# Three buffers for the second layer's operand sums and for raw weights, and six sums and two folds held to their written place on VectorE

## The chip, the cores and the metric

The kernel runs on one core of one Trainium2 chip. The metric is the device time of one execution in microseconds, as the median of several runs. Engines are called by the profile's names: PE (TensorE), DVE (VectorE), ACT (ScalarE), POOL (GpSimd) and SP (SyncE, which here only issues transfers).

## The reference, cut to what matters

Four batches, eight heads, 576 tokens, head size 64. An attention onto 32 packed tokens and back gives x (2304 x 512). Two feed-forward layers follow:

```python
def _moe_ref(x, w_in, w_out):              # 512 -> 2048 -> 512
    h = x @ w_in
    g = np.maximum(h, 0.0) + np.log1p(np.exp(-np.abs(h)))
    return (g @ w_out).astype(np.float32)

def _moe2_ref(x, w_gate, w_val, w_out):    # 512 -> 1536 -> 512
    gate = 1.0 / (1.0 + np.exp(-(x @ w_gate)))
    val = x @ w_val
    return (gate * val @ w_out).astype(np.float32)
```

The activations are float32. The five weight matrices arrive as 64-bit floats, 8 bytes an element.

## The kernel before, in words

**Stages.** Attention units (batch, group of four heads) run at the head of the program, mixed with the first chunks of layer 1. Layer 1 goes over entries (batch, chunk of 256 hidden columns): `emit_h` computes a chunk of h, `emit_out1` multiplies it with w_out, and DVE adds the product into `xa`, the resident activation (line 682). The last chunks are done for batches 0 and 1 first, then for 2 and 3. Layer 2 goes over two passes of two batches each (`ps` 0 and 1) and, in each, over 12 steps `f` of 128 hidden columns: `emit_gv` computes gate and value, `emit_out2` multiplies them with the output weights for two steps together and DVE adds the product into `xa` (line 1030).

**Products.** Every float32 operand is cut into a high part (rounded by ACT or POOL, `hi_of` and `split`) and a low part (x minus the high part, `split_lo`, line 101, on DVE or POOL), and a product is three matmuls (`mm3`, lines 113 to 115). In layer 2 a 2 x 2 block scheme with seven products is used: on the activation's side the seven operands are A11, A12, A22 (quarters of x) and S1 to S4 (sums of quarters). `prep_A(b)` makes them for batch b: a sum on DVE (`sum_` and `tt`, line 711), its high part on ACT (line 737), its low part on DVE or POOL (`ALO`), and so on. For batches 0 and 1 the chain is S1 = x21 + x22, S2 = S1 - x11, S4 = x12 - S2, S3 = x11 - x21. For batches 2 and 3 `fold_A` first writes two of the sums into `xa` in place (two instructions a batch), and `prep_A` then makes three more (S3, S1, S4). `prep_A(0)` and `prep_A(1)` are written into the end of layer 1, `fold_A(2)` and `fold_A(3)` into steps f = 3 and f = 5 of pass 0 or just behind them, `prep_A(2)` and `prep_A(3)` into the end of pass 0.

**The buffer of the sums.** A sum goes into a tile with the tag "sum" of the pool `w2[0]`, which has one buffer for it. S2 and S4 of batches 0 and 1 are written in place into the tile that holds S1.

**Raw weights.** A block of weights (512 KB) is loaded by SP into a tile of the pool `raw`, which has `NRAW` = 2 buffers (`load_next`), and DVE turns it into float32 by three integer instructions (`convert`, lines 180, 185, 189). Each conversion writes the next load into the program behind it; four loads are written at the start. `prep_B` prepares the weights of one step of layer 2: three conversions, four block sums on POOL (lines 800 to 803), splits, and four or five transfers that keep the blocks for pass 1 (line 816). Pass 1 reads them back (line 835).

**Order.** Background work (`jobs`) is written in small steps between the matmul groups by `tick`. The order on each engine and on SP isn't the written one, though: the framework plans it before the run from its own estimate of durations, and an instruction whose operands and buffer are free may be placed ahead of work written before it. `keep_in_program_order` ties an instruction behind the one written just before it on its engine, and makes it wait for nothing else. At run time each engine executes its list strictly in order.

Of the kernel before, what the change touches and what calls it, by code (L numbers as in the profile page):

```python
# [9 lines left out]
F32 = mybir.dt.float32  # L10
# [4 lines left out]
ALU = mybir.AluOpType  # L15
# [6 lines left out]
def attn_moe_moe_kernel(  # L22
# [21 lines left out]
    nc = tc.nc  # L44
# [5 lines left out]
    P = 128  # L50
    NC = 6
    CT = S // NC
    HS = S // 2
# [1 line left out]
    NCH1 = F1 // CF  # L55
    NCH2 = F2 // CF
    KD = DM // P
    NRAW = 2
    CPS = 1
    CPC = (1, 2)  # L60
    TP = 1
# [18 lines left out]
    big = ctx.enter_context(tc.tile_pool(name="big", bufs=11))  # L80
    raw = ctx.enter_context(tc.tile_pool(name="raw", bufs=NRAW))
    cv = ctx.enter_context(tc.tile_pool(name="cv", bufs=NCV))
# [17 lines left out]
    def split_lo(eng, lo, x, hi):  # L100
        eng.tensor_tensor(lo, x, hi.bitcast(F32), op=ALU.subtract)  # L101
# [599 lines left out]
    w2 = []  # L701
    NF = NCH2 * 2
    HB = B // 2
    Aop, Bop, scratch, gv = {}, {}, {}, {}

    def quarters(b):
        x1, x2_ = x2(b, 0), x2(b, 1)
        return x1[:, :2], x1[:, 2:], x2_[:, :2], x2_[:, 2:]

    def tt(to, x, y, op):  # L710
        nc.vector.tensor_tensor(to, x, y, op=op)

    def fold_A(b):

        x11, x12, x21, x22 = quarters(b)
        tt(x21, x21, x22, ALU.add)
        yield
        tt(x21, x21, x11, ALU.subtract)
        yield

    def prep_A(b):

        pool = w2[0] if b % 2 == 0 else big
        n = 11 if pool is big else 7
        Aop[b] = {}
        for nms in (("A11", "S2"), ("S3", "S1"), ("A12", "A22"), ("S4",)):
            tiles = [
                pool.tile([P, 2, 2, HS], F32R, tag="big", bufs=n, name="aop")
                for _ in range(len(nms))
            ]  # L730
            for e, nm in enumerate(nms):
                Aop[b][nm] = [tiles[0][:, e], tiles[-1][:, 1 if len(nms) == 1 else e]]
        x11, x12, x21, x22 = quarters(b)

        def split(nm, x):
            hi, lo = Aop[b][nm]
            nc.scalar.activation(hi, x, AF.Copy)  # L737
            split_lo(nc.gpsimd if nm in ALO[b] else nc.vector, lo, x, hi)

        def sum_(x, y, op, to=None):  # L740
            if to is None:
                to = w2[0].tile([P, 2, HS], F32, tag="sum", name="sum")
            tt(to, x, y, op)
            return to

        if b >= HB:

            steps = [
                ("A11", x11), ("S2", x21), ("S3", x22, x21, ALU.subtract),
                ("S1", x21, x11, ALU.add), ("A12", x12), ("A22", x22),  # L750
                ("S4", x12, x21, ALU.subtract),
            ]
            for nm, *x in steps:
                if len(x) > 1:
                    x = [sum_(*x)]
                    yield
                split(nm, x[0])
                yield
            return
        for nm, x in (("A11", x11), ("A12", x12), ("A22", x22)):  # L760
            split(nm, x)
            yield
        t = sum_(x21, x22, ALU.add)
        yield
        split("S1", t)
        yield
        sum_(t, x11, ALU.subtract, t)
        yield
        split("S2", t)
        yield  # L770
        sum_(x12, t, ALU.subtract, t)
        yield
        split("S4", t)
        yield
        t = sum_(x11, x21, ALU.subtract)
        yield
        split("S3", t)
        yield
# [101 lines left out]
    for i, (b, c) in enumerate(entries):  # L880
# [10 lines left out]
        if c >= 2 and b % 2 == 0:  # L891
# [3 lines left out]
            if k + 1 < len(groups):  # L895
                x, cc = groups[k + 1]
# [12 lines left out]
        for x in range(2):  # L909
            if (b, c) == (x + 2, NCH1 - 2):  # L910
                jobs.append((f"A{x}", prep_A(x)))
# [139 lines left out]
    for i, (ps, f) in enumerate(steps):  # L1051
        finish(f"B{ps}{f}")
        if i + 1 < len(steps):
            n_ps, n_f = steps[i + 1]
            jobs.append((f"B{n_ps}{n_f}", prep_B(n_ps, n_f)))
        if ps == 0 and f in FOLD:
            jobs.append((f"F{FOLD[f]}", fold_A(FOLD[f])))
        whole = list(range(HB))
        first_last = f in (SPL if ps else (SP0 + [NF - 1]))
        for n, group in enumerate([[p] for p in whole] if first_last else [whole]):  # L1060
            for p in group:
                finish(f"A{HB * ps + p}")
            emit_gv(ps, f, group)
            if ps == 0 and f == NF - 1:
                jobs.appendleft((f"A{HB + n}", prep_A(HB + n)))
            some_out2(LEFT if n or not first_last else LEFT0)
        if f % 2:
            todo.extend((ps, f // 2, t) for t in range(NTT))
            spread[0] = -DEL
# [37 lines left out]
```

## Time and profile before

| | |
|---|---|
| median of 3 runs | 865.22 us (864.93 to 866.91) |
| profiled execution, its own time | 869.49 us |
| its span, first to last instruction | 867.7 us |
| PE busy | 846.9 us, 98% |
| DVE busy | 587.9 us, 68% |
| POOL busy | 475.8 us, 55% |
| ACT busy | 339.8 us, 39% |
| mean granted clock of TensorE | 0.993 |

PE is busy nearly all the time, so what counts is where it stands still or is clocked lower, and which engine it waits for there. Layer 1 ends at about 439 us, pass 0 of layer 2 at about 642 us. Matmul ends are modelled by the profiler.

### The profile page before, as it was taken

What the parts mean: (1) busy time and instruction counts of PE and PEld (TensorE: products, weight loads), DVE (VectorE), ACT (ScalarE), POOL (GpSimd) and SP (SyncE); (2) the same over time, 40 slices, a digit from 0 to 9 for tenths busy, and PEclk for the clock granted to TensorE, in tenths of its full rate; (3) what the DMA queues carried; (4) which work ended last, traced back from release to release, by engine and by line L of the source; (5) the groups of instructions that cost most, each with busy time, mean ns of one, the idle gap of its engine ahead of it and who ended that gap; (6) DMA issues with size and microseconds to landing.
All of it is one profiled execution on the core that took longest, in us unless ns stands there. A gap on an engine that the chain in (4) does not pass through costs nothing.

```text
span 867.7 us, 15523 instructions
## 1 busy us (share of the span) xinstructions
PE 846.9 (98%) x6112; PEld 794.4 (92%) x6112; DVE 587.9 (68%) x1004; ACT 339.8 (39%) x626; POOL 475.8 (55%) x453
## 2 busy tenths in 40 slices
PE   7899999999999999999899999999999999999997
PEld 5789989999999999999889999999988999999996
DVE  1785566956365646646788687887897746667665
ACT  4367665554433434444433332222352432322210
POOL 4364333245655545575669786876984634436400
PEclk9899999999999999999999999999999999999999
DMA  9974321203033402400054655744515413213003
GB/s 227 209 207 117 83 56 29 74 25 99 1 98 92 135 12 87 127 26 1 1 177 146 188 152 149 207 132 128 163 51 151 115 47 90 67 43 110 13 1 109
DMA packets 58023, 85.53 MB, mean 99 GB/s; under 512 B 6368, under 2 KB 39264, under 8 KB 57952
## 3 DMA queue, kind: packets, MB, share of 16 engines
q1 hardware_dynamic: 56944, 83.31, 34.3%
q10 hardware_dynamic: 1008, 1.25, 0.4%
q8 instruction: 48, 0.79, 0.4%
q14 instruction: 23, 0.19, 0.1%
HBM read 65.67 MB, written 18.87 MB: 97 GB/s over the span
## 4 chain that ended last, share of the span: by engine, by line
PE 83%; DVE 8%; DMA 3%; ACT 2%; POOL 2%; issue 2%; SPq 0%; POOLq 0%; ACTq 0%; DVEq 0%
PE bank L115 8%; PE bank L113 8%; PE bank L114 8%; PE ps L674 7%; PE ps L675 7%; PE ps L677 7%; PE ps L1022 5%; PE ps L1023 5%; PE ps L1024 5%; PE ps L113 4%; PE ps L115 4%; PE ps L114 4%; PE ps L603 2%; PE ps L478 2%; PE ps L362 1%
## 5 line engine op out<-in xcount | busy, mean ns | idle before, releaser
L113 PE MATMUL bank<-aop,BH 128*128 128x288 f32 x672 | 199.2, 296 | 3.0 <-DVE work L987 1.1
L115 PE MATMUL bank<-aop,BL 128*128 128x288 f32 x672 | 198.9, 296 | 0.0
L114 PE MATMUL bank<-aop,BH 128*128 128x288 f32 x672 | 198.0, 295 | 0.2 <-DVE aop L101 0.2
L682 DVE TENSOR_TENSOR xa<-xa,ps 128x288 f32<-128x288 f32 x224 | 100.3, 451 | 105.8 <-PE ps L677 105.4
L101 POOL TENSOR_TENSOR ghl<-g,ghl 128x576 fp32r<-128x576 f32 x64 | 93.3, 1458 | 134.7 <-ACT ghl L108 125.2
L674 PE MATMUL ps<-ghl,woh 128*128 128x288 f32 x512 | 149.6, 307 | 2.6 <-DVE xa L682 2.4
L675 PE MATMUL ps<-ghl,wol 128*128 128x288 f32 x512 | 144.4, 297 | 0.0
L113 PEld LDWEIGHTS bank<-aop,BH 128*128 128x128 f32 x672 | 126.3, 188 | 8.7 <-issue 2.1
L114 PEld LDWEIGHTS bank<-aop,BH 128*128 128x128 f32 x672 | 126.6, 188 | 4.1 <-DVE aop L101 0.4
L115 PEld LDWEIGHTS bank<-aop,BL 128*128 128x128 f32 x672 | 126.6, 188 | 0.2 <-POOL BL L101 0.2
L101 POOL TENSOR_TENSOR BL<-cv,BH 128x512 fp32r<-128x512 f32 (+1 forms) x96 | 118.2, 1246 | 3.6 <-ACT BH L108 2.4
L677 PE MATMUL ps<-ghl,woh 128*128 128x288 f32 x512 | 109.5, 295 | 0.0
L674 PEld LDWEIGHTS ps<-ghl,woh 128*128 128x128 f32 x512 | 97.0, 189 | 5.1 <-ACT aop L737 2.1
L675 PEld LDWEIGHTS ps<-ghl,wol 128*128 128x128 f32 x512 | 97.2, 190 | 0.6
L975 DVE TENSOR_TENSOR work<-work,bank 128x576 f32<-128x576 f32 (+1 forms) x100 | 70.8, 724 | 30.7 <-PE bank L115 29.8
L1022 PE MATMUL ps<-oh,gv 128*128 128x512 f32 x216 | 84.5, 391 | 1.0 <-DVE xa L1030 0.5
L1023 PE MATMUL ps<-ol,gv 128*128 128x512 f32 x216 | 85.0, 393 | 0.0
L1024 PE MATMUL ps<-oh,gv 128*128 128x512 f32 x216 | 84.9, 394 | 0.0
L677 PEld LDWEIGHTS ps<-ghl,woh 128*128 128x128 f32 x512 | 82.7, 189 | 0.0
L1030 DVE TENSOR_TENSOR xa<-xa,ps 128x512 f32<-128x512 f32 x90 | 61.5, 684 | 28.8 <-PE ps L1024 28.4
L113 PE MATMUL ps<-A2h,wph 128*128 128x288 f32 x256 | 77.6, 303 | 0.3 <-ACT wph L587 0.3
L115 PE MATMUL ps<-A2h,wpl 128*128 128x288 f32 x256 | 76.3, 298 | 0.4 <-DVE wpl L101 0.4
(131 smaller groups left out, 1594.5 us busy)
## 6 DMA issues: line engine op xcount, KB each, us to landing
cv<-B SPq DMA_DIRECT2D x52, 256.0 KB, 2.7
B<-cv SPq DMA_DIRECT2D x48, 256.0 KB, 4.0
raw_in<-in_moe_w_in_dram SPq DMA_DIRECT2D x16, 512.0 KB, 3.9
raw_out<-in_moe_w_out_dram SPq DMA_DIRECT2D x16, 512.0 KB, 3.6
raw_g<-in_moe_w_gate_dram SPq DMA_DIRECT2D x12, 512.0 KB, 4.1
raw_v<-in_moe_w_val_dram SPq DMA_DIRECT2D x12, 512.0 KB, 4.5
raw_o<-in_moe_w_out_dram SPq DMA_DIRECT2D x12, 512.0 KB, 4.1
xa<-in_q_dram SPq DMA_DIRECT2D x6, 576.0 KB, 6.9
```

The source lines that it names most:

```text
L101: eng.tensor_tensor(lo, x, hi.bitcast(F32), op=ALU.subtract)
L113: nc.tensor.matmul(ps, wh, xh, start=first, stop=False)
L114: nc.tensor.matmul(ps, wh, xl, start=False, stop=False)
L115: nc.tensor.matmul(ps, wl, xh, start=False, stop=last)
L674: nc.tensor.matmul(out_, wh[:, ms], gh[:, f], start=f == 0, stop=False)
L675: nc.tensor.matmul(out_, wl[:, ms], gh[:, f], start=False, stop=False)
L677: nc.tensor.matmul(out_, wo_hl[c, f][0][:, ms], gl[:, f], start=False, stop=f == 1)
L682: nc.vector.tensor_tensor(dst, dst, out_, op=ALU.add)
L975: nc.vector.tensor_tensor(to, x, y, op=ALU.add)
L1022: nc.tensor.matmul(bank, gh[:, ts_], oh, start=f == 0, stop=False)
L1023: nc.tensor.matmul(bank, gh[:, ts_], ol, start=False, stop=False)
L1024: nc.tensor.matmul(bank, gl[:, ts_], oh, start=False, stop=f == 1)
```

## The change

The tag "sum" gets three buffers and every sum a tile of its own (S2 and S4 are no longer in place); `raw` gets three buffers. The six sums of `prep_A(2)` and `prep_A(3)` and the four instructions of `fold_A` are tied behind the instruction written before them on DVE; the sums of batches 0 and 1 aren't. A scratch area that the framework sets aside in SBUF for the descriptors of transfers issued by POOL is cut to 1024 bytes a partition; 4096 + 2 x 2304 bytes a partition are needed for the new buffers.

```diff
-    NRAW = 2
+    NRAW = 3
...
-    def tt(to, x, y, op):
-        nc.vector.tensor_tensor(to, x, y, op=op)
+    def tt(to, x, y, op, pin=True):
+        ins = nc.vector.tensor_tensor(to, x, y, op=op)
+        if pin:
+            tc.keep_in_program_order(ins)
...
-        def sum_(x, y, op, to=None):
-            if to is None:
-                to = w2[0].tile([P, 2, HS], F32, tag="sum", name="sum")
-            tt(to, x, y, op)
+        def sum_(x, y, op):
+            to = w2[0].tile([P, 2, HS], F32, tag="sum", bufs=3, name="sum")
+            tt(to, x, y, op, b >= HB)
             return to
...
-        sum_(t, x11, ALU.subtract, t)
+        t = sum_(t, x11, ALU.subtract)
...
-        sum_(x12, t, ALU.subtract, t)
+        t = sum_(x12, t, ALU.subtract)
...
-    nc = _bacc.Bacc("TRN2", target_bir_lowering=False, num_devices=1)
+    nc = _bacc.Bacc("TRN2", target_bir_lowering=False, num_devices=1, dynamic_dma_scratch_size=1024)
```

## Rows read from the trace of the kernel before

**Rows 1.** Windows: stretch, length, busy us of PE, PEld, DVE, ACT, POOL, clock, DMA share, GB/s.
```profile
0.00:20.00 20.00, 14.33 (x81) 9.60 (x82) 3.14 (x8) 7.84 (x23) 9.26 (x17) 0.98 0.96 219
...
420.00:440.00 20.00, 17.14 (x115) 16.48 (x113) 15.82 (x30) 5.62 (x9) 11.28 (x9) 0.91 0.14 40
440.00:460.00 20.00, 18.80 (x138) 18.37 (x139) 18.10 (x28) 6.13 (x9) 16.67 (x19) 1.00 0.61 198
460.00:480.00 20.00, 19.64 (x134) 18.59 (x134) 17.56 (x27) 7.79 (x13) 19.83 (x22) 1.00 0.52 148
...
620.00:640.00 20.00, 19.04 (x112) 16.59 (x110) 18.12 (x30) 10.12 (x19) 15.93 (x12) 1.00 0.29 84
640.00:660.00 20.00, 19.30 (x127) 17.81 (x127) 19.25 (x27) 9.95 (x19) 19.49 (x15) 1.00 0.36 103
```
**Rows 2.** Timeline of PE: start, duration, instruction, in brackets idle before it and releaser.
```profile
427.67 0.40 PE L674 MATMUL ps<-ghl,woh 128*128 128x288 f32 x1 [0.44 <-DVE xa L682]
431.44 0.37 PE L674 MATMUL ps<-ghl,woh 128*128 128x288 f32 x1 [1.91 <-DVE xa L682]
...
454.43 0.37 PE L113 MATMUL bank<-aop,BH 128*128 128x288 f32 x1 [0.75 <-DVE work L987]
```
**Rows 3.** Window behind the longest of these stands (columns as in rows 1).
```profile
432.00:436.00 4.00, 4.00 (x21) 4.00 (x20) 3.59 (x9) 0.63 (x1) 2.20 (x2) 0.57 0.19 8
```
**Rows 4.** Timeline of DVE: the sums of batch 1.
```profile
402.36 0.76 DVE L711 TENSOR_TENSOR sum<-xa 128x576 f32<-128x576 f32 x1
...
421.91 0.80 DVE L711 TENSOR_TENSOR sum<-sum,xa 128x576 f32<-128x576 f32 x1
...
425.28 1.97 DVE L711 TENSOR_TENSOR sum<-xa,sum 128x576 f32<-128x576 f32 x1 [1.86 <-POOL aop L101]
...
429.57 0.76 DVE L711 TENSOR_TENSOR sum<-xa 128x576 f32<-128x576 f32 x1 [1.59 <-POOL aop L101]
```
**Rows 5.** Timeline of POOL: a layer-1 low part, then the low part of S4.
```profile
425.21 1.43 POOL L101 TENSOR_TENSOR ghl<-g,ghl 128x576 fp32r<-128x576 f32 x1
428.11 1.43 POOL L101 TENSOR_TENSOR aop<-sum,aop 128x576 fp32r<-128x576 f32 x1 [1.47 <-ACT aop L737]
```
**Rows 6.** Line 711 by form: count, duration ns min/median/max, first and last start us.
```profile
L711 DVE TENSOR_TENSOR sum<-xa x10: 744/758/1183, 389.5 to 648.4; 128x576 f32<-128x576 f32 x10
L711 DVE TENSOR_TENSOR xa<-xa x4: 745/927/1103, 440.5 to 462.4; 128x576 f32<-128x576 f32 x4
```
**Rows 7.** Timeline of DVE at the start of layer 2.
```profile
449.75 0.69 DVE L180 TENSOR_SCALAR ps<-raw_v 128x512 int32<-128x512 int32 x1 [1.63 <-DMA raw_v<-in_moe_w_val_dram]
...
467.23 0.74 DVE L711 TENSOR_TENSOR sum<-xa 128x576 f32<-128x576 f32 x1
```
**Rows 8.** Timeline of SP's issues at the same place.
```profile
434.64 0.33 SPq L155 DMA_DIRECT2D raw_o<-in_moe_w_out_dram  x1
...
439.87 5.17 SPq L816 DMA_DIRECT2D B<-cv  x3
445.14 0.39 SPq L157 DMA_DIRECT2D raw_v<-in_moe_w_val_dram  x1
```
**Rows 9.** Windows where the folds are written, and around prep_A(2) and prep_A(3).
```profile
622.00:660.00 38.00, 36.34 (x227) 32.66 (x226) 36.75 (x56) 18.63 (x36) 33.42 (x26) 1.00 0.30 86
484.00:546.00 62.00, 62.00 (x403) 58.18 (x402) 48.76 (x74) 17.92 (x29) 48.65 (x57) 1.00 0.54 163
```
**Rows 10.** Timeline of ACT in prep_A(2).
```profile
625.02 0.69 ACT L737 ACTIVATE aop<-sum 128x576 fp32r<-128x576 f32 x1 [1.72 <-PE bank L114]
```
**Rows 11.** Timeline of SP at the start of the program.
```profile
10.73 3.08 SPq L237 DMA_DIRECT2D xa<-in_k_dram  x1
23.15 0.35 SPq L155 DMA_DIRECT2D raw_out<-in_moe_w_out_dram  x1
```
**Rows 12.** Timeline of POOL and of PE: what that load of k feeds.
```profile
25.40 1.62 POOL L351 TENSOR_SCALAR x<-xa 96x768 f32<-96x768 f32 x2 [6.39 <-DMA xa<-in_k_dram]
...
35.39 0.41 PE L362 MATMUL ps<-ident,x 96*128 96x96 f32 x3
```

## The prediction, made before the changed kernel ran

> **What bounds the kernel now.** I read the windows of 20 us first. From 80 us to the last outputs PE is busy for nearly the whole of every window but those of the turn from layer 1 to layer 2 and those in which the operands of batches 2 and 3 are made. PE stands still for 2.86 us between 420 and 440 us (20 - 17.14), for 1.20 + 0.36 = 1.56 us up to 480 us and for 0.96 + 0.70 = 1.66 us between 620 and 660 us [rows 1]. Everywhere else after the start the change has nothing to win, whatever it does to buffers.
>
> Then the timeline of PE, for what each of these stands waits for. The first stretch has 0.44 and 1.91 us, both for DVE's additions of line 682, which empty the PSUM banks of layer 1 [rows 2]; the other half microsecond is the last such addition before layer 2 may take the banks, and stays. Behind the long stand the granted clock is 0.57 over four microseconds in which PE is busy throughout [rows 3], that is, most of them at the lower of the two levels. 4 x (1 - 0.57) = 1.72 us of work are lost there, more than most of the stands themselves.
>
> Then the timeline of DVE, for why those additions are late. DVE isn't short of work time there; it stands in its order. The sum S4 of batch 1 waited 1.86 us and the sum S3 1.59 us for POOL [rows 4], and the additions are queued behind them. POOL was making the low parts of S2 and S4, which read the one "sum" buffer: S4 is written in place over S2, and S3 needs the buffer back, which it gets when the low part that starts at 428.11 is done [rows 5]. Both waits are waits for a buffer, not for a value.
>
> Last, the start of layer 2: PE's largest stand of the second stretch is for DVE [rows 2], which stood 1.63 us for a load of raw weights [rows 7]. The four instructions of the folds run there too, between 440.5 and 462.4 us [rows 6], and a sum of batch 2 at 467.23 [rows 7]. They are written some 40 to 160 us later in the program and were placed ahead because their operands are ready.
>
> **The change, part by part.** *Sums of batches 0 and 1.* With a tile of its own each, S4 no longer waits for POOL's low part of S2, nor S3 for that of S4. The operands of S1 were ready at 402.36, when its sum ran [rows 4], and S2 and S4 need only quarters of the same x; they may run from about then on, and S3 takes the tile that S1 leaves. Removed: 1.86 + 1.59 us of DVE standing still, with it PE's 0.44 + 1.91 = 2.35 us, and, if no other stand comes there, the low clock's 1.72 us. Sum -4.07. ACT's high parts behind these sums come earlier too, and with them the last low parts of layer 1 on POOL. What is late next is the last addition of line 682, the half microsecond that stays. Bounds: 0, if the planner leaves both sums behind POOL's work, and -4.58, if that half microsecond goes as well (2.86 + 1.72).
>
> *Raw weights.* A third tile lets each load go out one conversion earlier. At 434.64 SP issues the first load that waited for a free tile; the load of v for the second step goes out only at 445.14, behind three transfers that keep blocks for pass 1 and hold SP for 5.17 us [rows 8]. One tile earlier it goes out where its predecessor went, ahead of these three, and DVE's 1.63 us disappear. *The folds, at their place of origin:* four instructions with a median of 0.93 us [rows 6] and the sum of 0.74 [rows 7], together some 4.4 us, leave a stretch in which DVE is busy 18.10 and 17.56 of 20 us [rows 1]. The two together take away more DVE time than PE waits there, 1.56 us. I take -1.5. Bounds: 0, if the step becomes bound by POOL (19.83 of 20 us busy between 460 and 480 [rows 1]), and -1.56.
>
> *The folds, at their new place.* Pass 0 runs from 440 to 642 us in 12 steps, 16.8 us each; the folds stand behind the background work of f = 3 and f = 5, so between about 490 and 541 us, or a little later. In 484 to 546 us PE is busy 62.00 of 62 us and DVE 48.76 [rows 9]; the four instructions lie in the remaining 13 us. Cost 0. If that cover were gone it would be their whole duration, 4 x 0.927 = 3.7.
>
> *The sum of batch 2 that goes back.* It joins the five sums that already lie in 622 to 660 us. DVE is busy 36.75 of 38 us there while PE lost 38 - 36.34 = 1.66 us [rows 9]: here DVE is the bound, and another instruction is paid for by PE. The ten sums from xa take 0.744 to 1.183 us [rows 6]; I take 0.8. The extra buffers give nothing back, since the sums are tied behind the low part written before them and DVE has next to no idle time to fill. Bounds: -1.66, if the new order suits PE and its stands there go, and +1.97, the longest sum in the trace [rows 4].
>
> The Trainium skill speaks against this part: "SBUF — State Buffer", section "Who interferes with whom", says that a VectorE instruction with two SBUF inputs and a GpSimd instruction that reads SBUF exclude each other for the whole of the one that came first. The trace agrees as far as it goes: the sum of 1.97 us started at 425.28, 0.07 us after a POOL instruction of 1.43 us [rows 4, 5], while the shortest sum took 0.744 [rows 6]. By that rule a sum put beside a POOL instruction of 1.43 us costs up to 0.74 + 1.43 = 2.2, and the total would be 1.4 us worse than by my 0.8.
>
> *The start.* The third raw load has a free tile at once, so it goes out ahead of the load of k that SP issues at 10.73, no longer at 23.15 [rows 11]. The transfers run at 219 GB/s there with the DMA engines busy 0.96 [rows 1], so 512 KB put that k back by about 524,288 / 219,000 = 2.4 us. POOL was waiting for it (6.39 us, until 25.40), but PE takes the transposes of that unit only at 35.39 [rows 12], with 27.0 as the end of POOL's part: 8.4 us of cover. Cost 0. With the cover gone it is +2.4; a conversion that comes earlier can win at most what one late load costs, -1.63.
>
> *The scratch area.* The view of transfers lists only SP and ACT as issuers, so nothing uses it: 0, and a loss of anything would need a transfer from POOL.
>
> Sum: -4.07 - 1.5 + 0 + 0.8 + 0 = -4.77. The profiled execution took 869.49 us, with a span of 867.7; it becomes 864.7 (span 862.9). It lies 4.27 us above the median of the runs shown, 865.22, and I take the same difference off the median: 860.45, say 860.5.
>
> **The rivals.** *Given back by the next bound.* The first stretch is freed, but PE then asks for the operands of the second step four microseconds sooner, and POOL, which makes them, is the busiest engine beside PE there; the 1.5 is not won. The sum in 622 to 660 us stands beside POOL's work and costs 2 us. For it: POOL's 19.83 of 20 [rows 1]; against it: POOL's input comes from DVE, which is freed by 3.45 us just before. -4.07 + 0 + 2.0 = -2.1: 863.1, within 0.3%. The exclusion that the Trainium skill ("SBUF — State Buffer", "Who interferes with whom") states is this rival's second half. Chance 0.20.
>
> *The sums stay where they are.* The change doesn't do what it says in the place that counts: the planner, which thinks POOL's low parts early enough, leaves the sums and the additions in the old order, and DVE still waits in it, now for ACT or PE. Only the raw weights and the folds work: -1.5 + 0.8 = -0.7: 864.5. Against it: S1 was placed at 402.36, far ahead of its split, as soon as its buffer was free [rows 4]. Chance 0.08.
>
> *Slower: the tied sums hold DVE.* A tied sum may not pass the low part written before it, and that low part waits for ACT's high part, which waits for PE to give back an operand buffer: 1.72 us in the one case that the trace shows [rows 10]. If DVE stands at each of the six tied sums as long, with the additions and products that PE needs queued behind it, it costs 6 x 1.72 = 10.3, less the 5.57 won elsewhere: +4.7, 870.0. It decides from 8.2 us on (5.57 + 2.6). Against it: in the old order DVE has next to no idle time in the same stretch, with the same low parts before the same sums [rows 9]. Chance 0.10.
>
> **How the numbers follow.** A measurement of this kernel tells about 0.3%, 2.6 us, from no change. My forecast has 0.62, with a range of its own from 858.5 to 862.5, nearly all faster. The first rival's upper part (up to -2.6) adds 0.05 to faster; the rest of it and the second rival are the same; the third is slower. Faster 0.67, same 0.23, slower 0.10. The range: below, the lower bounds of the two first terms and a win at the start together and nothing paid for the sum of batch 2 (-4.58 - 1.56 - 1.63 = -7.8, 857.4), rounded to 857.0; above, it takes in the first two rivals, and ends at 866.0, where the third begins.
>
> **What would show it.** Right: no wait of the sums for POOL at line 711, the three sums of batch 1 close behind 402 us, no stand of PE above 0.6 us and a clock of 1.00 between 420 and 440 us; raw_v issued ahead of the three transfers; PE busy 19.8 or more of 20 us up to 480 us; the folds between 484 and 546 us with PE still full; PE's loss in the stretch of prep_A(2) and prep_A(3) at about 2.5 us. Wrong: a new stand of PE for POOL's BL or for ACT at the second step; DVE idle in front of a tied sum; or PE waiting for unit 2's transposes near 35 us. What would make the number wrong above all is the clock: the 1.72 us are won only if no stand of similar length comes in the same stretch.

## The result, and the profile after

The changed kernel takes 870.77 us (median; 869.55 to 875.92), the kernel before, on the same chips, 866.87 us. The ratio is 1.0052, with a 95% interval of 1.003 to 1.0073: slower by about 4 us, where 860.5 was forecast. The profiled execution of after took 869.78 us, with a span of 868.0.

The windows of 20 us of after (columns as in [rows 1]):
```profile
20.00:40.00 20.00, 15.88 (x194) 13.67 (x195) 16.79 (x39) 8.74 (x24) 9.50 (x10) 1.00 1.09 255
...
420.00:440.00 20.00, 19.45 (x148) 19.22 (x147) 17.52 (x33) 6.67 (x11) 14.70 (x15) 1.00 0.25 73
440.00:460.00 20.00, 19.99 (x151) 19.78 (x150) 19.04 (x30) 7.17 (x11) 19.83 (x24) 1.00 0.80 247
460.00:480.00 20.00, 19.06 (x127) 17.71 (x126) 13.45 (x20) 8.45 (x15) 16.81 (x17) 1.00 0.33 105
...
620.00:640.00 20.00, 19.35 (x120) 17.24 (x119) 17.48 (x28) 8.51 (x18) 14.28 (x12) 1.00 0.22 59
640.00:660.00 20.00, 16.68 (x97) 14.87 (x96) 19.61 (x24) 8.23 (x15) 14.22 (x11) 0.91 0.29 79
```
Where the forecast saw a gain there is one: PE is busy 19.45 and 19.99 of 20 us between 420 and 460, where it had 17.14 and 18.80 [rows 1], at a clock of 1.00. The loss is at 640 to 660, with 16.68 of 20 and a clock of 0.91, and at the start, with 15.88. The first of these stretches in the kernel before, in the profile of [rows 1] and in a second one (e4 below):
```profile
20.00:40.00 20.00, 18.53 (x207) 16.55 (x205) 13.60 (x36) 8.29 (x24) 5.92 (x7) 0.85 1.00 239
20.00:40.00 20.00, 17.72 (x209) 14.95 (x206) 16.30 (x44) 9.28 (x27) 8.27 (x10) 1.00 0.99 236
```

The sums of batch 1 on DVE's timeline in after:
```profile
402.25 0.76 DVE L711 TENSOR_TENSOR sum<-xa 128x576 f32<-128x576 f32 x1
403.05 1.05 DVE L711 TENSOR_TENSOR sum<-sum,xa 128x576 f32<-128x576 f32 x1
404.13 1.73 DVE L711 TENSOR_TENSOR sum<-xa,sum 128x576 f32<-128x576 f32 x1
...
417.79 0.76 DVE L711 TENSOR_TENSOR sum<-xa 128x576 f32<-128x576 f32 x1 [0.96 <-POOL aop L101]
```
Three of them stand directly behind one another at 402 us, and the waits of 1.86 and 1.59 us of [rows 4] are down to one of 0.96 which nothing on PE follows. Of PE's stands at line 682 only the last addition's is left (timeline of PE):
```profile
437.22 0.40 PE L113 MATMUL bank<-aop,BH 128*128 128x288 f32 x1 [0.55 <-DVE xa L682]
```
The load of v goes out ahead of the three transfers that it stood behind in [rows 8] (timeline of SP):
```profile
443.68 0.38 SPq L157 DMA_DIRECT2D raw_v<-in_moe_w_val_dram  x1
444.45 4.94 SPq L817 DMA_DIRECT2D B<-cv  x3
```
DVE doesn't wait for it, and the folds are where they are written (timeline of DVE; compare [rows 6, 7]):
```profile
451.25 0.69 DVE L180 TENSOR_SCALAR ps<-raw_v 128x512 int32<-128x512 int32 x1
...
487.03 2.61 DVE L711 TENSOR_TENSOR xa<-xa 128x576 f32<-128x576 f32 x2
...
522.42 1.64 DVE L711 TENSOR_TENSOR xa<-xa 128x576 f32<-128x576 f32 x1
...
525.38 0.75 DVE L711 TENSOR_TENSOR xa<-xa 128x576 f32<-128x576 f32 x1
```
At the start, POOL's timeline in after:
```profile
27.64 1.62 POOL L351 TENSOR_SCALAR x<-xa 96x768 f32<-96x768 f32 x2 [9.37 <-DMA xa<-in_k_dram]
29.23 1.26 POOL L101 TENSOR_TENSOR wol<-cv,woh 128x512 fp32r<-128x512 f32 x1
31.07 1.20 POOL L496 TENSOR_TENSOR a<-a,m 96x384 f32<-96x384 f32 x1 [0.58 <-DVE m L495]
...
36.91 1.26 POOL L101 TENSOR_TENSOR wol<-cv,woh 128x512 fp32r<-128x512 f32 x1 [1.56 <-ACT woh L108]
38.13 1.62 POOL L496 TENSOR_TENSOR a<-a,m 96x384 f32<-96x384 f32 x2
```
and PE's beside it:
```profile
39.01 0.47 PE L506 MATMUL ps<-ident,a 96*128 96x96 f32 x3 [2.14 <-POOL a L496]
```
The k that was put back arrives 2.24 us later than in [rows 12], as forecast. But the raw_out weights that now arrive before it have their low parts ("wol") made on POOL, and these stand ahead of attention's multiplications of line 496, for which PE waits. Behind this wait the granted clock is at the lower of its two levels for a part of the next microseconds, which costs 8 x (1 - 0.79) = 1.7 us of work:
```profile
38.00:46.00 8.00, 6.67 (x45) 5.71 (x46) 5.37 (x11) 4.17 (x12) 4.24 (x6) 0.79 0.79 209
```

Last, DVE's timeline where the operands of batches 2 and 3 are made:
```profile
629.96 2.52 DVE L101 TENSOR_TENSOR aop<-xa,aop 128x576 fp32r<-128x576 f32 x2
632.41 0.44 DVE L976 TENSOR_TENSOR work<-work,bank 128x288 f32<-128x288 f32 x1
632.78 0.98 DVE L711 TENSOR_TENSOR sum<-xa 128x576 f32<-128x576 f32 x1
...
642.89 1.84 DVE L711 TENSOR_TENSOR sum<-xa 128x576 f32<-128x576 f32 x1
...
645.85 1.37 DVE L711 TENSOR_TENSOR sum<-xa 128x576 f32<-128x576 f32 x1
...
650.22 1.96 DVE L711 TENSOR_TENSOR sum<-xa 128x576 f32<-128x576 f32 x1
```
and PE's:
```profile
645.50 0.40 PE L113 MATMUL bank<-aop,BH 128*128 128x288 f32 x1 [0.77 <-ACT aop L739]
649.01 0.61 PE L114 MATMUL bank<-aop,BH 128*128 128x288 f32 x1 [1.97 <-DVE aop L101]
```
Behind the longer of these stands the clock is at the lower level as well, 4 x (1 - 0.58) = 1.7 us:
```profile
648.00:652.00 4.00, 2.99 (x12) 2.99 (x13) 4.00 (x4) 0.00 (x0) 3.56 (x3) 0.58 0.43 131
```

**Where the time went, stage by stage.** The table is worked out from starts of instructions in the timelines of each kernel's profiled execution, in us. Layer 1 has 64 units, one for each batch, chunk and half of the tokens. A: from the span's start to ACT's table load ahead of the function of the 17th unit (line 646). B: from there to the function of the 56th. C, the turn of the layers: from there to layer 2's first matmul of a BL operand (line 115). D: steps 1 and 2 of pass 0. E: step 3. F: from the last step of pass 0 to the second step of pass 1, where the operands of batches 2 and 3 are made. The edits of e1 to e16 are told below; e4 is the kernel before once more.

| kernel | A | B | C | D | E | F |
|---|---|---|---|---|---|---|
| before | 184.02 | 202.03 | 54.35 | 23.94 | 16.05 | 36.96 |
| e4 | 180.09 | 202.16 | 53.33 | 24.00 | 16.05 | 37.06 |
| after | 185.32 | 201.93 | 50.34 | 22.55 | 16.47 | 41.83 |
| e1 | 186.39 | 201.82 | 50.31 | 22.73 | 20.25 | 37.29 |
| e2 | 185.94 | 201.85 | 50.24 | 22.54 | 16.47 | 37.25 |
| e3 | 184.07 | 201.76 | 50.27 | 24.47 | 16.93 | 41.41 |
| e6 | 183.85 | 202.20 | 50.22 | 24.54 | 16.45 | 37.25 |
| e7 | 185.37 | 201.85 | 53.30 | 23.02 | 25.37 | 36.85 |
| e8 | 180.64 | 201.91 | 53.29 | 25.95 | 15.99 | 41.23 |
| e9 | 184.57 | 201.95 | 50.33 | 22.83 | 16.33 | 42.07 |
| e10 | 185.06 | 201.95 | 50.33 | 22.54 | 16.53 | 43.85 |
| e11 | 183.12 | 201.86 | 50.29 | 22.46 | 16.61 | 37.30 |
| e13 | 184.11 | 201.85 | 50.28 | 22.53 | 16.53 | 37.28 |
| e14 | 183.32 | 201.94 | 50.24 | 22.67 | 16.38 | 39.99 |
| e15 | 183.11 | 201.91 | 50.32 | 22.46 | 16.57 | 37.32 |
| e16 | 181.01 | 201.91 | 50.35 | 22.54 | 16.49 | 37.34 |

After against e4: A +5.23, B -0.23, C -2.99, D -1.45, E +0.42, F +4.77, and -0.83 in the step behind F (20.31 to 19.48): +4.92, which is the difference of the spans, 868.0 - 863.1. In kernels that are alike there, all columns but A repeat within some 0.6 us, except C of before, which has the low clock of [rows 3]. A does not: the kernel before has 184.02 and 180.09 in its two profiles. A part of that is the clock as well: over the first two windows of 20 us it is 0.98 and 0.85 in the first profile and 0.91 and 1.00 in the second, 3.4 and 1.8 us lost; the rest is not explained. So the size of A is taken from ratios of times below.

### The profile page after: what moved, and what is told of

Same layout as the page of the kernel before. It is cut to its first block, busy times and chain, and to the rows that moved or that the text cites. A ratio compares the mean times of both kernels' runs of the same rounds, so it can differ in the third digit from the quotient of the medians.

```text
span 868.0 us, 15525 instructions
## 1 busy us (share of the span) xinstructions
PE 846.4 (98%) x6112; PEld 793.2 (91%) x6112; DVE 592.3 (68%) x1004; ACT 341.1 (39%) x626; POOL 473.1 (55%) x453
## 4 chain that ended last, share of the span: by engine, by line
PE 87%; POOL 5%; DVE 4%; DMA 2%; ACT 1%; issue 1%; SPq 0%; POOLq 0%; DVEq 0%; ACTq 0%
PE bank L115 9%; PE bank L113 9%; PE bank L114 9%; PE ps L674 7%; PE ps L677 7%; PE ps L675 7%; PE ps L1025 6%; PE ps L1024 5%; PE ps L1023 5%; PE ps L113 4%; PE ps L115 4%; PE ps L114 4%; PE ps L603 2%; PE ps L478 2%; PE ps L362 2%; POOL BL L101 1%
## 5 line engine op out<-in xcount | busy, mean ns | idle before, releaser
L104 POOL TENSOR_SCALAR BH<-cv 128x512 fp32r<-128x512 f32 (+1 forms) x48 | 27.9, 590 | 91.8 <-PE bank L114 91.8
L976 DVE TENSOR_TENSOR bank<-work,bank 128x576 f32<-128x576 f32 (+1 forms) x75 | 55.2, 737 | 33.3 <-PE bank L115 32.8
```

What stands on the lines that cost most here:

```text
L976: nc.vector.tensor_tensor(to, x, y, op=ALU.add)
```

## The experiments

Ratios are to the kernel before on the same chip, with 95% intervals; 0.001 is 0.87 us. The edits are against the changed kernel unless it says otherwise.

**e1: no ties.**
```
-    def tt(to, x, y, op, pin=True):
+    def tt(to, x, y, op, pin=False):
...
-            tt(to, x, y, op, b >= HB)
+            tt(to, x, y, op)
```


> The changed kernel with nothing tied: three sum buffers and three raw buffers, folds and sums free to be placed early. Theory 1 (the ties cost the time where the operands of batches 2 and 3 are made): three sums of batch 2 leave the crowded stretch, PE's distance from the twelfth step of pass 0 to the second step of pass 1 falls from 41.8 us in the changed kernel to 37 or less (36.96 in the kernel before), and the time is 4 us or more below that of the changed kernel, at a ratio of about 0.997 to the kernel before. Theory 2 (the extra buffers themselves disturb that stretch, the ties do nothing): the distance stays above 40 us and the ratio at 1.005. The folds come back to the start of layer 2 and cost at most 1 us there.

Measured: 1.0055 [1.0041, 1.0068], as slow as the changed kernel, but for another reason: F is back at 37.29, and E has grown to 20.25. The four folds and three sums of batch 2 now run there (464 to 477 us), and PE waits 3.16 us for POOL.

**e2: folds tied, sums free.**
```
-            tt(to, x, y, op, b >= HB)
+            tt(to, x, y, op, False)
```


> The changed kernel with the folds still tied and the six sums free. Theory 1: the sums are the harmful ties, so the stretch of batches 2 and 3 is as fast as without any tie, and the start of layer 2 keeps the gain of the folds' leaving it: ratio 0.994 to 0.997 to the kernel before, and up to 1 us below the kernel with nothing tied. Theory 2: as the changed kernel, 1.005. If the folds' ties are the harmful ones instead, this kernel is slow and the one with nothing tied is fast.

Measured: 1.0008 [0.9996, 1.0021], not the 0.994 to 0.997 of the first theory; E 16.47, F 37.25. So freeing the six sums gives back 0.0044, 3.8 us, and F has it (4.6 in the profiles), and the ties of the folds are worth the 3.8 us of E that e1 lost. In this window of e2 PE doesn't stand any more:
```profile
640.00:660.00 20.00, 20.00 (x132) 18.84 (x132) 17.14 (x21) 6.84 (x13) 14.72 (x13) 1.00 0.44 128
```

**e3: two raw buffers again, the rest as changed** (`NRAW = 2`).

> The changed kernel with two raw buffers in place of three. In the changed kernel's trace the third raw load goes out ahead of a load of k, and layer 1 then runs 1.5 us later than in the kernel before. Theory 1: with two buffers that 1.5 us is gone, the stretch of batches 2 and 3 stays slow: 1.5 us below the changed kernel, ratio about 1.003. Theory 2 (the raw buffer disturbs the late stretch too): 4 us below, ratio 1.000 or less. Rival 3: the raw buffer's gain at the start of layer 2 is worth as much as it costs at the start: no difference.

Measured: 1.0039 [1.0022, 1.0056]. D is 24.47 with two raw buffers and 22.55 with three: the third one is worth 1.9 us at layer 2. Yet the kernel without it isn't slower, so the third buffer costs at least as much elsewhere; A is the only column that is left.

**e4: the kernel before, once more.**

> The kernel before once more, for its granted clock and span in every run: its profiled execution was 2.6 us above the median of ten runs. Ratio 1.000. If the low clock behind the stand of PE at 431 us is there in some runs and not in others, the runs' clocks spread by 0.002 and their times by 1.7 us with them; if it is there in all, the clock of the fast runs is no higher than the 0.993 of the profiled one.

Measured: 1.0 [0.999, 1.0011]. It shows what a profile of an unchanged kernel can differ by: 3.9 us in A and 1.0 in C. The low clock of [rows 3] is not there (1.00 between 420 and 440 us), though PE's stand of 1.89 us for DVE's addition is; over whole executions of this run the clock is 0.996 to 1.000. POOL's order at the start, for comparison with after:
```profile
28.25 0.83 POOL L496 TENSOR_TENSOR a<-a,m 96x384 f32<-96x384 f32 x1 [3.04 <-DVE m L495]
30.94 1.27 POOL L101 TENSOR_TENSOR wol<-cv,woh 128x512 fp32r<-128x512 f32 x1 [1.86 <-ACT woh L108]
32.16 1.05 POOL L496 TENSOR_TENSOR a<-a,m 96x384 f32<-96x384 f32 x1
...
35.73 1.62 POOL L496 TENSOR_TENSOR a<-a,m 96x384 f32<-96x384 f32 x2 [1.72 <-DVE m L494]
```
One wol ahead of the multiplications at 35.73, not two, and this one early.

**e6: e2 with two raw buffers** (`NRAW = 2`, sums free).

> Three sum buffers, the folds tied, the sums free, two raw buffers. Theory 1 (the third raw buffer costs some 5 us at the start, where the kernel before typically starts its first chunk of layer 1 at 42.4 us, and gains 1.5 at the start of layer 2; the ties of the sums cost 4; the sum buffers gain 3): start as the kernel before, turn of the layers -3.0, first three steps of layer 2 +0.5 to +1.4, operands of batches 2 and 3 -0.6: -2 us, ratio 0.9975. Rival 2 (the late start of the changed kernel is chance of the clock, not the raw buffer): no better than the same kernel with three raw buffers, which had 1.0008.

Measured: 0.9962 [0.9945, 0.9979]: 3.3 us faster than the kernel before, most of it column C. Against e2 it is 4.0 us faster, although D is 2.0 slower: the third raw buffer's price at the start is about 6 by this pair, and about 3 by the pair of after and e3 (1.1 net, 1.9 in D and 0.5 in E, less 0.4 in F). The granted clock goes with it: its median over whole executions is 0.999 in e6 and 0.994 in e2, 0.996 in e3 and 0.992 in after. As an estimate, 0.001 of a span of 868 us is 0.87 us, so 4.3 and 3.5 us of these prices are clock.

**e7: the kernel before with the third raw buffer and the scratch size alone.**
```
-    NRAW = 2
+    NRAW = 3
...
-    nc = _bacc.Bacc("TRN2", target_bir_lowering=False, num_devices=1)
+    nc = _bacc.Bacc("TRN2", target_bir_lowering=False, num_devices=1, dynamic_dma_scratch_size=1024)
```


> The kernel before with the third buffer for raw weights and the scratch size, nothing else. Theory 'the third buffer loses at the start what it wins at layer 2, and more' (start +3 to +5, first steps of layer 2 -1.5 to -1.9): ratio 1.002 to 1.004. Theory of the prediction (start 0, layer 2 -1.5 at most): 0.998 to 1.000.

Measured: 1.0143 [1.0117, 1.0169], 12.4 us slower; neither theory had that. A is +5.3 and D -1.0 against e4, about as the first theory said, but E is 25.37 instead of 16.05. The timeline of DVE there:
```profile
469.16 9.84 DVE L711 TENSOR_TENSOR xa<-xa 128x576 f32<-128x576 f32 x1
```
of POOL:
```profile
467.47 2.88 POOL L101 TENSOR_TENSOR gv<-work,gv 128x576 fp32r<-128x576 f32 x2
470.25 0.79 POOL L800 TENSOR_TENSOR cv<-cv 128x256 f32<-128x256 f32 x1
...
477.75 0.65 POOL L104 TENSOR_SCALAR oh<-cv 128x512 fp32r<-128x512 f32 x1
478.49 1.64 POOL L101 TENSOR_TENSOR ol<-cv,oh 128x512 fp32r<-128x512 f32 x1
```
and of PE:
```profile
482.21 0.58 PE L113 MATMUL bank<-aop,BH 128*128 128x288 f32 x1 [7.60 <-DVE work L975]
```
A fold whose fastest is 0.743 us took 9.84. From 467.47 to 478.40 (477.75 + 0.65) POOL's instructions follow one another without a gap; the first gap is the 0.09 us up to 478.49, and the fold ends 0.60 us behind its beginning. DVE's additions of line 975 are queued behind the fold, and PE stands 7.60 us for them; behind that the clock is 0.83 between 480 and 500 us. So a fold that is free to move is a risk, and how large a one depends on where the loads let it go: no loss that shows at 440 to 462 us [rows 6] (e6, with two raw buffers and the folds tied, has D and E no shorter than e4), 3.8 us in e1, 9.3 here.

**e8: the kernel before with the ties alone** (`tt` of after, one "sum" buffer, two raw buffers).

> The kernel before with the ties of folds and of the sums of batches 2 and 3 alone: one sum buffer, two raw buffers. Theory 'a tie makes the sums late, whatever the buffers' (+3.9 to +4.8 where the operands of batches 2 and 3 are made, nothing elsewhere): ratio 1.004 to 1.006. Theory 'the ties cost only together with the three sum buffers, since the order of the other sums then differs': 0.999 to 1.001.

Measured: 1.0069 [1.0043, 1.0095]. F is 41.23, as in after: the ties make the sums late whatever the buffers are. D is 25.95, 1.95 more than in e4, with PE stands of 2.15 and 1.01 us for DVE; why the ties cost there with one sum buffer and not with three (e3, 24.47) was not followed further.

**e9 and e10: one sum.** e9 frees S3 of batch 2 alone, e10 ties it alone.
```
-            tt(to, x, y, op, b >= HB)
+            tt(to, x, y, op, b >= HB and not (b == HB and x is x22))   # e9
+            tt(to, x, y, op, b == HB and x is x22)                     # e10
```


> The changed kernel with one tie less: the sum S3 of batch 2, the only one that lay outside the crowded stretch before, is free. Theory 1a (my prediction's term: this one sum, put back into the stretch, is what is paid): the distance from the twelfth step of pass 0 to the second step of pass 1 falls from 41.8 us to about 37.5, ratio about 1.001. Theory 1b (every tied sum stands late, behind an addition of layer 2 that waits for PE, and the chain of the later sums starts late with it): S1 of batch 2 is tied as before and comes as late, the distance stays at 40 us or more, ratio 1.004 or more.

> The counterpart: of the six sums only S3 of batch 2 is tied, and the folds; three raw buffers. Theory 1a: the distance is as in the changed kernel, 41 us or more, ratio 1.005. Theory 1b: the sum is late, but the others have their own buffers and need not wait for it, so the distance rises by no more than the work of one sum, from 37.25 to about 38.5, ratio 1.001 to 1.003.

Measured: e9 1.0042 [1.0027, 1.0058], F 42.07; e10 1.0061 [1.0039, 1.0084], F 43.85. One tie is enough: with S3 alone held, F is 2 us worse in the profile than with all six (the intervals of the times overlap), and freeing S3 alone moves the loss to the next tied sum. So it isn't the number of sums in the stretch (three in e2, five in the kernel before, with the same F).

**e14: all ties, but the sums of batch 2 are written earlier**, at the head of the last step of pass 0.
```
+        if ps == 0 and f == NF - 1:
+            sums_first(HB)          # S3, S1, S4 of batch 2, tied
...
-                    x = [sum_(*x)]
+                    x = [presum.pop((b, nm)) if (b, nm) in presum else sum_(*x)]
```


> The changed kernel, all ties kept, but the three sums of batch 2 are written at the head of the last step of pass 0, ahead of its gv, and no longer inside the job that makes the operands. Theory 'lateness' (the ties cost because that job is written late, so that DVE's work for batch 2 is pushed into the stretch of batch 3): the operands of batches 2 and 3 give back most of their 3.9 us, as in e2: ratio 1.000 to 1.002. Theory 'a tie as such' (a fixed order on DVE is worse than a planned one, wherever the sum is written): 1.004 to 1.006.

Measured: 1.0031 [1.0019, 1.0043], between the two; F 39.99, so 1.84 of the 4.58 us between after and e2 come back. DVE's sums:
```profile
613.96 4.70 DVE L711 TENSOR_TENSOR sum<-xa 128x576 f32<-128x576 f32 x3
...
634.05 0.98 DVE L711 TENSOR_TENSOR sum<-xa 128x576 f32<-128x576 f32 x1
...
638.23 0.75 DVE L711 TENSOR_TENSOR sum<-xa 128x576 f32<-128x576 f32 x1
...
639.98 1.85 DVE L711 TENSOR_TENSOR sum<-xa 128x576 f32<-128x576 f32 x1
```
and PE's one stand above 0.4 us behind 630 us:
```profile
643.78 0.40 PE L114 MATMUL bank<-aop,BH 128*128 128x288 f32 x1 [1.15 <-DVE aop L101]
```
With the same ties at another place the loss is smaller, so the place counts. It isn't shown to be all: the three sums in a row took 4.70 us, those of batch 3 are tied as before, and the clock is 1.00 behind this stand, where after lost 1.7 us to it.

**e12 and e16: e2 with the first low parts of raw_out on DVE.**
```
-        split_lo(nc.gpsimd, lo, x, hi)
+        split_lo(nc.vector if key[:2] == ("out", 0) else nc.gpsimd, lo, x, hi)
```


> The kernel of e2 (folds tied, sums free, three raw buffers), with one edit: the low parts of the first raw_out weights of layer 1 ("wol" of chunk 0) are made on DVE and no longer on POOL, so that they can't stand ahead of attention's multiplications of line 496. The order of the loads stays that of e2, with raw_out ahead of k. Theory 'POOL order' (the start loses what PE waits for POOL's late multiplications): the start wins back most of its 3 to 5 us, ratio 0.995 to 0.997. Theory 'load order' (the start loses because k comes 2.24 us later): no change against e2, 1.000 to 1.002. If DVE is itself full there, the multiplications' inputs from DVE come later and it is worse, 1.003.

> The kernel of e12 once more, for its profile. Theory 'POOL order': attention's multiplications of line 496 stand without wol between them on POOL, k still comes at about 27.5 us, PE's wait of 2.14 us for POOL near 39 us is gone, and the 17th chunk of layer 1 starts at 181 to 183.5 us (185.9 in e2). Theory 'load order': the chunk starts at 185 to 186.

Measured: 0.9962 [0.9947, 0.9976] in both; the profile is read from e16. That is 4.0 us less than e2, with A at 181.01 instead of 185.94. POOL at the start of e16:
```profile
25.90 2.20 POOL L351 TENSOR_SCALAR x<-xa 96x768 f32<-96x768 f32 x2 [8.22 <-DMA xa<-in_k_dram]
29.30 0.83 POOL L496 TENSOR_TENSOR a<-a,m 96x384 f32<-96x384 f32 x1 [1.20 <-DVE m L495]
32.01 0.87 POOL L496 TENSOR_TENSOR a<-a,m 96x384 f32<-96x384 f32 x1 [1.88 <-DVE m L495]
...
35.61 1.62 POOL L496 TENSOR_TENSOR a<-a,m 96x384 f32<-96x384 f32 x2 [1.76 <-DVE m L494]
```
The multiplications have no wol before them, and PE's longest wait for them is 0.98 us, not 2.14. Here k is still 2.33 us later than in e4 (23.57), and A is within 1 us of e4's. The order of the loads costs next to nothing; POOL's order, which follows from it, costs the rest, and most of that by the clock: its median over whole executions is 0.999 in both runs and 0.994 in e2, 4.3 us by the estimate above. In the stretch that costs after 1.7 us, e16 has
```profile
38.00:46.00 8.00, 7.56 (x58) 5.86 (x55) 7.05 (x12) 6.87 (x20) 3.85 (x5) 1.00 0.97 260
```

**e13: e2 with the fourth raw load made after attention of batch 0.**
```
-    for _ in range(4):
+    for _ in range(3):
         load_next()
...
+    load_next()
     jobs.append(("wp00", prep_wp_one(0, 0)))
```


> The kernel of e2 (folds tied, sums free, three raw buffers), with only three of the four first calls of the raw loads made at the start, and the fourth made after attention of batch 0. The first raw_out still goes out ahead of k, the second one five loads later, so that only one low part of raw_out weights stands ahead of attention's multiplications on POOL instead of two. Theory 'POOL order': about half of the start's loss comes back, ratio 0.997 to 0.999. Theory 'load order': k is as late as in e2, 1.000 to 1.002.

Measured: 0.999 [0.9971, 1.0008], 1.6 us less than e2, with one wol ahead of the multiplications instead of two. The direction of 'POOL order'; the two intervals overlap.

**e11: e2 with the third raw buffer handed over late.** A small tile takes it until attention's pools are released, so that the loads of the start go out as with two buffers.
```
+    held = raw.tile([P, KD * P, 2], I32, tag="raw", name="held")
+    held = held[:, 0, :].bitcast(F32)
+    nc.gpsimd.memset(held, 0.0)
+    freed = cst.tile([P, 2], F32, name="freed")
...
         if (b, c) == (1, 2):
             att.release()
+            tc.keep_in_program_order(
+                nc.gpsimd.tensor_scalar(freed, held, 1.0, 0.0, op0=ALU.mult, op1=ALU.add)
+            )
```


> As the kernel with the folds tied, the sums free and three raw buffers, but the third raw buffer is taken by a small dummy (one memset and one read on GpSimd) until the first chunk of layer 1 behind the attention. Theory 1: the start is that of the kernel before (first chunk of layer 1 near 42.4 us in a usual execution), and the gains stay: -3.0 at the turn of the layers, -1.5 + 0.4 in the first steps of layer 2, -0.6 in batches 2 and 3: -4.5 us, ratio 0.995. Rival 2 (the start is chance): 1.0008 as with the third buffer from the beginning.

Measured: 859.97 us, 0.9928 [0.9905, 0.995]: the fastest kernel of the study, and faster than both. It has C 50.29, D 22.46 and F 37.30 at once, with POOL's order at the start as in e4.

**e15: e11 and the edit of e12 together.**

> The kernel of e11 (folds tied, sums free, third raw buffer handed over after the start) with the edit of e12 as well (low parts of the first raw_out weights on DVE). If what e12 won is only what POOL's order had cost, e11 has it already, and the ratio stays at 0.992 to 0.994. If POOL held the start in the kernel before too, it is 0.988 to 0.991.

Measured: 0.9964 [0.9951, 0.9977]. Nothing is won over e11, and by the ratios 3 us are lost, though no column of the table differs by more than 0.05. In the profile PE has a stand for POOL's multiplications that e11 doesn't have, with a clock of 0.89 between 30 and 46 us (1.00 in e11; the A of e11 has a clock of 0.85 between 20 and 40 instead):
```profile
38.80 0.47 PE L511 MATMUL ps<-ident,a 96*128 96x96 f32 x3 [1.52 <-POOL a L501]
```
Whether POOL held the start in the kernel before stays open, since the edit brings a stand of its own.

## Why the prediction was wrong

The net sign was wrong by two terms of the sum that were priced near nothing, the sum of batch 2 and the start. In both the prediction left out a stand of PE and, behind the stand, the clock. The two large terms were right.

- *Sums of batches 0 and 1*: the mechanism is right, and C lost 3.0 us against e4 (53.33 to 50.34), as in every kernel with the sum buffers. The forecast -4.07 had the low clock's 1.72 us of [rows 3] in it, which three of the four profiles with one sum buffer (e4, e7, e8; C 53.29 to 53.33) don't have: mis-sized by one execution's clock. Against the profile that it was read from, C lost 4.01, but the sum took the 1.72 off the median of the runs too, and this profile lay 4.27 us above that median. In e4 the stand for the last addition is 1.01 us, and 0.55 in after, which is most of what C won beside the 2.33 us of the two stands that the forecast named.
- *Raw weights*: right, -1.45 to -2.0 in D. What the prediction doesn't say is that with the third buffer the folds must be tied: left free they land in step 3, where POOL is full, and cost 3.8 us (e1) or 9.3 (e7). The price at their place of origin was read from [rows 6], where they cost 0.93 each; another order of loads puts them elsewhere.
- *The folds at their new place*: right; PE has 20.00 of 20 us from 480 to 500. Step 3 pays 0.4 (E), where PE waits for POOL: of "Given back by the next bound" that is all that came.
- *The sum of batch 2 that goes back*, +0.8, is the main step that failed: it is +3.9 (F +4.77, the step behind it -0.83), twice the upper bound of 1.97. The step counted one more sum at its duration. But the tie also held S3 of batch 2 at 632.78, directly behind an addition of layer 2, with its low part at 634.60, against 623.06 for the free sum's low part in e2. DVE, which had "next to no idle time" [rows 9], was idle 2.5 us of 620 to 640 instead (17.48 of 20 busy; 19.90 in e2), and had four of the six sums and their low parts left for 640 to 660, where PE waits for them. Of the 3.9, 2.2 are longer standing (PE stands 3.97 us of 620 to 660, 1.79 in e4), and 1.7 the low clock behind the stand of 1.97. The clock alone isn't the cause: e3 has it at 1.00 there and stands 4.64 us. e2, e8, e9 and e10 show that the ties do it, one being enough; e14 points to a part of the place in the program.
- *The start*, 0, is the second failed step: +3 to +6 by the pairs of times. k was late as forecast, and the cover of 8.4 us held for it. What the step left out is the load that took k's place: with it, two low parts of 1.26 us stand on POOL ahead of attention's multiplications, and PE waits 2.14 us for these. Behind this wait the clock falls. All seven profiles with the wait (after, e1, e2, e7, e9, e10, e14; 2.14 or 2.15 us) have a clock of 0.66 to 0.83 between 36 and 46 us, 1.7 to 3.4 us of work; e15, with 1.52 us, has 0.83; the eight others have 1.00. Four of these eight (before, e3, e6, e11) have a low clock earlier instead, 0.66 between 18 and 28 us, but e6 and e11 have a median of 0.999 over whole executions, so most of theirs don't. e16 gives both back with k still late; e13 points the same way.
- *The clock over the whole execution* is the sign that the prediction named for a wrong number, but it looked for it between 420 and 440 us alone. Its median is 0.992 in the ten runs of after and 0.997 to 0.999 in those of the kernel before on four chips: 4 to 6 us by the estimate above, as much as the whole loss. By this count the standing that the change removes and the standing that it adds come out about even.
- *Scratch area*: not tried by itself. e7 has it together with the third raw buffer, and A to F account for its time.

Of the rivals, *Slower: the tied sums hold DVE* had the outcome (870.0) and the place, but only half its mechanism: DVE did lose time ahead of the ties, but 2.5 us and not six waits of 1.72, and no tied sum shows a wait for a low part. The rest of the loss was at the start, so that its number came out is luck. The chance of 0.10 was too low above all because two things that the change does at once, ties and an earlier load, were each judged by the trace of an order that they alter.

## What to carry to other kernels

An extra buffer at the head of a queue of loads changes the order of work on every engine that converts what is loaded: follow the load to its consumers and ask what is queued behind them there, not only which load it displaces. Where a new stand of some 2 us appears, look at the clock behind it, and price that too. A tie fixes an instruction behind everything written before it that waits; where it is written decides what it costs, and freeing or tying is best tried edit by edit, since here the folds had to be tied and the sums free. Of this change the sum buffers, the folds' ties and a third raw buffer that stays out of the start are worth 0.7% together, the whole as given costs 0.5%.

## What the runs showed of the hardware

That a DVE instruction with two SBUF inputs can take far longer than one instruction of POOL beside it: 9.84 us for a fold whose fastest is 0.743, beside a run of POOL instructions without a gap (e7). The Trainium skill, "SBUF — State Buffer", section "Who interferes with whom", says that such an instruction contends with a GpSimd instruction that reads SBUF, and that the ports they share are an exclusive lock. e7 agrees with the exclusion, but shows it over about a dozen of POOL's instructions in a row. That a gap of 0.09 us between two of these let the fold in is read from one place, and was not tested by itself.

That a stand of PE of about 2 us is followed by a lower clock in some places and not in others. Seven profiles have it behind a wait of 2.14 or 2.15 us near 39 us; behind the stand of 1.89 to 1.91 us for the addition of line 682, one profile has it [rows 3] and three don't (e4, e7, e8). So a profile of one execution can hold or miss some microseconds of it, and times have to be compared over several runs.
